# Half chunk's casts, masks, state sums and a gated load in the first stretch of a retention and mixer kernel

## The chip, the cores and the metric

The kernel runs on one core of a Trainium2 chip. Time is device time in microseconds (us) of that core. Executions of one kernel differ by up to 0.9% on one chip even at full clock.

## What it must compute

Retention (linear attention with a decay per head) for 8 batches, 8 heads, 576 rows, head size 64, and a token and channel mixer on its result.

```python
# attention: q, k, v are [8, 8, 576, 64]
scores = scale * q @ k^T
Dmat   = where(rel >= 0, gamma[h] ** rel, 0)          # rel = row - column
x      = ((scores * Dmat) @ v), heads joined          # [8, 576, 512]
# mixer
h  = (x^T @ U) @ V                                    # rank 32, over the rows
u  = x + h^T
out = u + relu(u @ w_ch1) @ w_ch2                     # 512 -> 2048 -> 512
```

## The kernel before

The batches are taken in pairs. A pair's 1152 rows make nine chunks of 128; chunk `J` is the **half chunk**, which has the last 64 rows of one batch and the first 64 of the next. The first pair has its own code, because nothing can be overlapped with it yet: its rows are taken as four **units** of 256 rows and two halves of the half chunk. The second pair starts with the "third batch"; its chunks come by the usual route: load, cast, transpose by DMA (`DMA_TRANSPOSE qkT<-qk`).

Names used below: `scale_u` and `cast_u` cast and scale a unit's queries, keys or values; `T_u` transposes them; `SC_u` makes scores, `SC_off` those between the two halves of a unit, `mask_u` masks them; `RV_u` multiplies with the values; `ST_u` adds to the running state, `Sblk` evicts it; `QS_u` multiplies queries with the state; `XS_u` scales the result. A **y item** is a group of matmuls of the first channel product (`u @ w_ch1`) with its evictions; PE has a list of them as filler. w1 and w2 stand for the weights `w_ch1` and `w_ch2`. `warm(n)` issues matmuls that only keep TensorE busy.

Three engine lists matter. ScalarE (ACT) does the evictions of transposed operands in the startup, GpSimd (POOL) casts and issues the weight loads, SyncE (SP) issues all other loads and the transposes.

```python
    def load(pr, i, which):
        c = ch.setdefault((pr, i), {})
        for j in which:
            if ("f", j) not in c:
                c["f", j] = stage.tile([P, H, D], FP32, tag="stage", name="stage_t")
            ...
                nc.sync.dma_start(out=c["f", j][rows, :, :], in_=...)
    ...
    def startup():
        load_u(0, (1, 0)) ...            # the loads of units 0, 1 and the half chunk
        warm(10)
        cast_unit(0)
        ...
        SC_u(0, 0, ps_sc, "psc")
        mask_u(0, 0)
        cast_unit(1)
        ...
        T_u(1, 1, nc.scalar)
        SC_u(0, 1, ps_o, "po")
        mask_u(0, 1)
        SC_off(0, ps_sc, "psc")
        warm(3)
        T_u(1, 0)
        nc.vector.memset(sblk, 0.0)
        SC_off(1, ps_o, "po")
        warm(3)
        SC_u(1, 0, ps_sc, "psc")
        mask_u(1, 0)
        cast_J(0, nc.scalar, nc.vector)  # half chunk: keys on ScalarE, queries on VectorE
        SC_u(1, 1, ps_o, "po")
        mask_u(1, 1)
        ...
        load_w1(10, 14)                  # 512 KB of w_ch1
        scale_u(3, 0, nc.gpsimd)         # unit 3's queries: scale and cast
        for hh in range(2):
            cast_u(3, 0, hh, nc.gpsimd)
        load_w1(14, 16)                  # the last 256 KB
        for hh in range(2):
            cast_u(3, 2, hh, nc.gpsimd)
        ...
    def first_stretch():
        ...
        for g in range(NI, NI + 4):      # the third batch's first 11 loads
            load(*order[g], (1, 0, 2) if g < NI + 3 else (1, 0))
        unit(2, (0, 1, 2), False)
        y(2)
        unit(3, (2, 3), True)
        for f in range(0, NF, 2):
            load_w2(f)                   # 2 MB of w_ch2
        ...
```

Of the kernel before, what the change touches and what calls it, by code (L numbers as in the profile page):

```python
# [34 lines left out]
def kernel(  # L35
# [81 lines left out]
    def early_consts():  # L117
        scratch = y1_pool.tile([P, NF, 4 * P], BF16, tag="y10", name="y1")
        un[0]["off"] = scratch[:, 0:4, :].rearrange("p (a x) (y i) -> p a (x y) i", x=2, i=P)
        tri = scratch[:, 4, 0:P]  # L120
        make_identity(nc, ident)
        nc.gpsimd.memset(lnb, math.log(scale))
        nc.gpsimd.iota(
            posU, pattern=[[2 * P, 4], [1, 2], [0, H]], base=0, channel_multiplier=2,
            allow_small_or_imprecise_dtypes=True,
        )
        nc.gpsimd.iota(
            iotaU, pattern=[[-1, 2], [1, P]], base=0, channel_multiplier=-2,
            allow_small_or_imprecise_dtypes=True,
        )  # L130
        nc.gpsimd.iota(
            pos, pattern=[[P, NI], [0, H]], base=0, channel_multiplier=1,
            allow_small_or_imprecise_dtypes=True,
        )
        nc.gpsimd.iota(
            posJ, pattern=[[-2 * J * P, 2], [0, H]], base=2 * J * P, channel_multiplier=1,
            allow_small_or_imprecise_dtypes=True,
        )
        make_upper_triangular(nc, tri, val=1.0, diag=True)
        nc.gpsimd.memset(triJ, 0.0)  # L140
        nc.gpsimd.affine_select(
            out=triJ, in_=triJ, compare_op=ALU.is_gt, fill=1.0, base=0,
            pattern=[[-2, HALF]], channel_multiplier=1)
        for h in range(H):
            nc.vector.memset(lngt[:, :, h], lng[h])
        nc.scalar.activation(out=Af[:, 0, 0:H], in_=lngt[:, 0, :], func=AF.Exp)
        nc.vector.tensor_copy(out=fan, in_=ident[0:R, None, 0:R].to_broadcast([R, 4, R]))
        nc.vector.tensor_scalar_add(posU[:, 2:4], posU[:, 2:4], -float(4 * P - HALF))
        nc.vector.tensor_tensor(
            out=posU.rearrange("p u j h -> p (u j) h"),  # L150
            in0=lngt[:, 0:8, :], in1=posU.rearrange("p u j h -> p (u j) h"), op=ALU.mult)
        nc.scalar.activation(out=vscaleU, in_=posU, func=AF.Exp, bias=lnb, scale=-1.0)
        nc.vector.tensor_scalar(
            out=posJ, in0=posJ, scalar1=0.5, scalar2=None, op0=ALU.mult)
        nc.vector.tensor_tensor(out=posJ, in0=posJ, in1=lngt[:, 0:2, :], op=ALU.mult)
        nc.scalar.activation(out=vscaleJ, in_=posJ, func=AF.Exp, bias=lnb, scale=-1.0)
        nc.scalar.activation(out=posJ, in_=posJ, func=AF.Exp, bias=0.0, scale=1.0)
        nc.vector.tensor_scalar(
            out=triU[0:HALF], in0=iotaU[0:HALF], scalar1=0.0, scalar2=None, op0=ALU.is_ge)
        nc.vector.tensor_scalar(  # L160
            out=triU[HALF:P], in0=iotaU[HALF:P], scalar1=-float(P), scalar2=None,
            op0=ALU.is_ge)
        nc.vector.tensor_scalar_add(pos[:, J + 1:NI, :], pos[:, J + 1:NI, :], -float(S))
        nc.vector.tensor_scalar_add(pos[HALF:P, J, :], pos[HALF:P, J, :], -float(S))
        nc.vector.tensor_tensor(out=lngt, in0=lngt, in1=pos, op=ALU.mult)
        nc.scalar.activation(out=qscale, in_=lngt, func=AF.Exp, bias=0.0, scale=1.0)
        nc.scalar.activation(out=vscale, in_=lngt, func=AF.Exp, bias=lnb, scale=-1.0)
        nc.vector.tensor_copy(out=triH[0:HALF], in_=tri[0:HALF, 0:HALF])
        nc.vector.tensor_copy(out=triH[HALF:P], in_=tri[HALF:P, HALF:P])
        nc.vector.memset(U_E[:, J, :], 0.0)  # L170
        nc.vector.memset(U_O[0:HALF, 0, :], 0.0)
        nc.vector.memset(V4[:, 0:HALF], 0.0)
        nc.vector.memset(V4[:, HALF + S:], 0.0)
        nc.vector.tensor_copy(out=swap[:, 0:HALF], in_=ident[:, HALF:P])
        nc.vector.tensor_copy(out=swap[:, HALF:P], in_=ident[:, 0:HALF])

    def load_u_rows():
        nc.sync.dma_start(
# [53 lines left out]

    ch = {}

    def load(pr, i, which):
        c = ch.setdefault((pr, i), {})
        for j in which:
            if ("f", j) not in c:
                c["f", j] = stage.tile([P, H, D], FP32, tag="stage", name="stage_t")
            dram = (q, k, v)[j]  # L240
            for rows, b, t0 in parts(pr, i):
                n = rows.stop - rows.start
                nc.sync.dma_start(
                    out=c["f", j][rows, :, :],
                    in_=dram[b, :, t0:t0 + n, :].rearrange("h s d -> s h d"),
                )
# [383 lines left out]
    def cast_u(u, j, hh, eng):  # L630
        o, f = unit_views(u, j, hh)
        if eng is nc.scalar:
            nc.scalar.activation(out=o, in_=f, func=AF.Copy)
        else:
            eng.tensor_copy(out=o, in_=f)  # L635
# [145 lines left out]
    def zero_J(x, eng):  # L781
        for j in range(3):
            t = stage.tile([P, H, D], FP32, tag="stage", name="stage_t")
            hj[x]["f", j] = t
            if eng is nc.scalar:
                nc.scalar.activation(
                    out=t.rearrange("p h d -> p (h d)"),
                    in_=ident[:, None, :].to_broadcast([P, 4, P]), func=AF.Copy, scale=0.0)
            else:
                eng.memset(t, 0.0)  # L790
# [118 lines left out]
    def startup():  # L909
# [12 lines left out]
        cast_unit(0)  # L922
        T_u(0, 1, nc.vector)
        nc.vector.memset(un[0]["off"][HI], 0.0)
        zero_J(1, nc.vector)
        load_J(1, (1, 0, 2))
        load_u(2, (1, 0, 2))
# [7 lines left out]
        cast_unit(1)  # L935
        cast_u(0, 2, 0, nc.gpsimd)
        cast_u(0, 2, 1, nc.gpsimd)
        cast_u(1, 2, 0, nc.gpsimd)
        load_w1(0, 2)
        cast_u(1, 2, 1, nc.gpsimd)  # L940
        T_u(1, 1, nc.scalar)
        SC_u(0, 1, ps_o, "po")
        mask_u(0, 1)
        SC_off(0, ps_sc, "psc")
        warm(3)
        T_u(1, 0)
        nc.vector.memset(sblk, 0.0)
        SC_off(1, ps_o, "po")
        warm(3)
        SC_u(1, 0, ps_sc, "psc")  # L950
        mask_u(1, 0)
        cast_J(0, nc.scalar, nc.vector)
        SC_u(1, 1, ps_o, "po")
        mask_u(1, 1)

        acc1 = pss_tile()
        ST_u(0, ALL, acc1, True)
        Sblk(acc1, 1)
        RV_u(0, 0)
        RV_u(0, 1)  # L960
        RV_off()
        XS_u(0)
        T_J(0)
        acc2 = ps_big.tile([P, NHP, P], FP32, tag="big", name="pss2")
        ST_u(0, ALL, acc2, True)
        prep_vJ(0)
        cast_urows()
        RV_u(1, 0)
        SC_J(0)
        mask_J(0)  # L970
        ST_u(1, LO, acc1, False)
        Sblk(acc1, 2)
        cast_J(1, nc.gpsimd, nc.gpsimd)
        load_w1(2, 4)
        prep_vJ(1)
        load_w1(4, 6)
        scale_u(2, 0, nc.gpsimd)
# [4 lines left out]
        load_w1(8, 10)  # L982
        for hh in range(2):
            cast_u(2, 2, hh, nc.gpsimd)
        load_w1(10, 14)
        scale_u(3, 0, nc.gpsimd)
        for hh in range(2):
            cast_u(3, 0, hh, nc.gpsimd)
        load_w1(14, 16)
        for hh in range(2):  # L990
            cast_u(3, 2, hh, nc.gpsimd)
        RV_u(1, 1)
        QS_u(1, 0, 1)
        XS_u(1, 0, 1)
        ST_u(1, ALL, acc2, False)
        Sblk(acc2, 3)
        QS_u(1, 1, 2)
        XS_u(1, 1, 2)
        RV_J(0)
# [33 lines left out]
    def first_stretch():  # L1033
# [3 lines left out]
        def y(n):  # L1037
            for _ in range(n):
                fn = next(ys, None)
                if fn is not None:  # L1040
                    fn()
# [13 lines left out]

        def unit(u, slots, last):
            T_u(u, 1, nc.vector)
            if last:
                y(1)
            T_u(u, 0)  # L1060
            y(1)
            SC_u(u, 0, ps_sc, "psc")
            mask_u(u, 0)
            y(1)
            ST_u(u, LO, acc, False)
            Sblk(acc, slots[1])
            SC_u(u, 1, ps_sc, "psc")
            mask_u(u, 1)
            if not last:
                scale_u(3, 1, nc.vector)  # L1070
            y(1)
            if not last:
                ST_u(u, HI, acc, False)
                Sblk(acc, slots[2])
            RV_u(u, 0)
            QS_u(u, 0, slots[0])
            QS_u(u, 1, slots[1])
            if last:
                RV_J(1)
                XS_J(1)  # L1080
            RV_u(u, 1)
            XS_u(u)

        for g in range(NI, NI + 4):
            load(*order[g], (1, 0, 2) if g < NI + 3 else (1, 0))
        unit(2, (0, 1, 2), False)
        y(2)
        unit(3, (2, 3), True)
        nc.vector.memset(w2_sb[:, 0, 0:1], 0.0)
        for f in range(0, NF, 2):  # L1090
# [78 lines left out]
```

## Time and profile before

| | before |
|---|---|
| time, median (range) | 326.98 us (326.25 to 327.29), 3 runs |
| span of the profiled execution | 323.8 us |
| PE busy | 312.6 us, 97% |
| PE idle before 70 us | 6.8 us |

PE works 97% of the time, so only the first 70 us have anything to win. The prediction below shows the page's busy row and the order of time of PE, ScalarE and SyncE there. First the chain of waits that ended last, as the page sums it up, each engine with its share of the span:

```profile
PE 77%; ACT 4%; DVE 2%; DMA 1%; issue 1%; DVEq 0%
```

Hardly any transfer is on that chain (1%). Second, the table by stage between 36 and 40 us; after the window and its length come busy us (and instructions) of PE, PEld, DVE, ACT and POOL, then the granted clock, the DMA share and GB/s:

```profile
36.00:38.00 2.00, 1.60 (x15) 0.94 (x13) 0.69 (x1) 1.07 (x2) 0.00 (x0) 1.00 1.22 224
38.00:40.00 2.00, 1.26 (x10) 0.65 (x10) 0.72 (x1) 0.86 (x2) 1.78 (x3) 1.00 0.90 201
```

The DMA engines move over 200 GB/s all that time. Third, SyncE's order of time at the last of the eleven early third-batch loads (start, length, what it issues):

```profile
49.57 5.39 SPq L243 DMA_DIRECT2D stage_t<-in_q_dram  x1
```

Of the loads before it, those issued after 40 us took SyncE 0.8 to 2.1 us each. This one took 5.39; it is the only one that had four of the w2 loads (issued from 46.9 us on, every 0.7 us) ahead of it. PE's line where the third batch begins, without a wait:

```profile
66.71 0.32 PE L296 MATMUL pp<-qkT 64*64 64x64 bf16 x16
```

### The profile page before, as it was taken

To read this page: it belongs to the slowest core of one execution; us is meant where nothing else is said; L and a number is where in the kernel's file an instruction comes from. 1 tells how busy PE (TensorE), PEld (TensorE's weight loads), DVE (VectorE), ACT (ScalarE), POOL (GpSimd) and SP (SyncE) were. 2 spreads that over 40 slices of the span, in tenths; PEclk is the share of its full clock that TensorE was granted. 3 is DMA by queue.
4 is the path that set the end of the run, shared out by engine and by line. 5 is a ranking of instruction groups with operands and counts; after the bars stand their busy time and mean duration, and the time that the engine had idled before them with its cause. 6 is when DMAs were issued, how large, how long until landed. Compare 5 with 4: busy or idle time off the path is not lost.

```text
span 323.8 us, 9143 instructions
## 1 busy us (share of the span) xinstructions
PE 312.6 (97%) x3885; PEld 170.8 (53%) x3885; DVE 172.9 (53%) x342; ACT 146.1 (45%) x334; POOL 101.5 (31%) x172
## 2 busy tenths in 40 slices
PE   7899899999999999999999999999999999999996
PEld 3575545764444454457644454457644454467544
DVE  7867456229726577555844476556744475500012
ACT  6757547892020583058800583058800572047400
POOL 7796329223113723052221523052231500010000
PEclk9999999999999999999999999999999999999999
DMA  7999999999975999979997599959996340330022
GB/s 215 256 233 255 227 216 185 201 188 127 254 180 139 232 193 187 213 147 190 197 205 166 140 184 206 217 140 189 182 217 156 100 68 3 107 105 0 2 78 84
DMA packets 152904, 53.30 MB, mean 165 GB/s; under 512 B 132032, under 2 KB 150336, under 8 KB 152864
## 3 DMA queue, kind: packets, MB, share of 16 engines
q1 hardware_dynamic: 144512, 40.40, 68.1%
q0 software_dynamic: 8352, 12.32, 15.9%
q8 instruction: 30, 0.49, 0.7%
q14 instruction: 10, 0.08, 0.1%
HBM read 36.85 MB, written 9.44 MB: 143 GB/s over the span
## 4 chain that ended last, share of the span: by engine, by line
PE 77%; ACT 4%; DVE 2%; DMA 1%; issue 1%; DVEq 0%
PE ps_y L549 37%; PE ps_y L515 32%; PE pp L296 2%; DVE u L464 2%; ACT y L520 1%; DMA qkT<-qk 1%; PE pp L316 1%; PE pp L328 1%; PE ps_y L560 1%; PE AB L358 1%; PE pa L431 1%; PE ph L458 1%; ACT s_sb L373 1%; ACT qk L264 0%; ACT uT L489 0%
## 5 line engine op out<-in xcount | busy, mean ns | idle before, releaser
L515 PE MATMUL ps_y<-uT,w_sb 128*128 128x256 bf16 (+2 forms) x768 | 133.1, 326 | 1.8 <-ACT y L520 1.1
L520 ACT ACTIVATE y<-ps_y 128x384 bf16<-128x384 f32 (+2 forms) x192 | 89.7, 491 | 96.6 <-PE ps_y L515 95.8
L549 PE MATMUL ps_y<-w_sb,y 128*128 128x512 bf16 x560 | 126.5, 380 | 0.0
L515 PEld LDWEIGHTS <-w_sb 128*128 128x128 bf16 x768 | 72.1, 98 | 49.6 <-issue 3.7
L549 PEld LDWEIGHTS <-y 128*128 128x128 bf16 x560 | 52.6, 98 | 61.1
L272 POOL TENSOR_TENSOR vt<-stage_t,vscale 64x256 bf16<-64x256 f32 (+1 forms) x81 | 50.4, 622 | 63.8 <-DMA stage_t<-in_v_dram 51.8
L538 DVE TENSOR_TENSOR o_sb<-ps_y,u 128x512 f32<-128x512 f32 (+2 forms) x38 | 25.2, 664 | 81.7 <-PE ps_y L549 79.4
L541 POOL DMA_DIRECT2D out_dram<-o_sb x31 | 17.2, 555 | 103.7 <-DVE o_sb L538 100.0
L304 DVE TENSOR_TENSOR ret<-pp,triH 128x512 bf16<-128x512 f32 x27 | 18.7, 692 | 24.6 <-PE pp L328 19.1
L464 DVE TENSOR_TENSOR u<-ph,xt 128x768 bf16<-128x768 f32 (+2 forms) x24 | 21.8, 951 | 5.9 <-PE ph L458 4.2
L437 ACT ACTIVATE a_sb<-pa 128x128 bf16<-128x128 f32 x8 | 2.2, 278 | 43.7 <-PE pa L431 43.7
L344 DVE TENSOR_TENSOR xt<-pp,qscale 128x512 bf16<-128x512 f32 x27 | 18.6, 690 | 4.7 <-PE pp L328 4.2
L338 DVE COPY q<-qkT 64x256 bf16<-64x256 bf16 x48 | 13.1, 272 | 13.7 <-DMA qkT<-qk 12.7
L263 DVE CAST qk<-stage_t 64x256 bf16<-64x256 f32 x54 | 18.8, 347 | 1.2
L383 DVE TENSOR_TENSOR s_sb<-AB,Af 64x256 bf16<-64x256 f32 x42 | 17.7, 422 | 2.1 <-ACT s_sb L378 1.5
L264 ACT ACTIVATE qk<-stage_t 128x512 bf16<-128x512 f32 x27 | 16.8, 622 | 0.0
L635 POOL CAST qk<-stage_t 128x512 bf16<-128x512 f32 x16 | 10.2, 637 | 11.4 <-DMA stage_t<-in_q_dram 6.6
L376 ACT ACTIVATE Af<-AB 128x256 f32<-128x256 f32 x24 | 9.2, 385 | 7.8 <-PE AB L358 7.4
L261 ACT ACTIVATE qk<-stage_t 128x256 bf16<-128x256 f32 x27 | 11.1, 410 | 0.0
L692 DVE TENSOR_TENSOR ret<-psc,triU 128x1024 bf16<-128x1024 f32 x8 | 9.6, 1206 | 2.6 <-PE psc L684 2.6
L296 PEld LDWEIGHTS <-qkT 64*64 64x64 bf16 x432 | 5.6, 107 | 9.8 <-issue 8.0
L209 PE MATMUL pw<-ident 128*128 128x512 bf16 x26 | 7.8, 443 | 1.4 <-POOL ident masks.py:199 1.4
(134 smaller groups left out, 220.0 us busy)
## 6 DMA issues: line engine op xcount, KB each, us to landing
stage_t<-in_k_dram SPq DMA_DIRECT2D x32, 256.0 KB, 4.9
stage_t<-in_q_dram SPq DMA_DIRECT2D x32, 256.0 KB, 5.4
stage_t<-in_v_dram SPq DMA_DIRECT2D x32, 256.0 KB, 5.6
out_dram<-o_sb POOLq DMA_DIRECT2D x31, 256.0 KB, 3.5
w_sb<-in_moe_w_ch_dram POOLq DMA_DIRECT2D x14, 256.0 KB, 8.3
stage_t<-in_k_dram SPq DMA_DIRECT2D x8, 128.0 KB, 3.7
stage_t<-in_q_dram SPq DMA_DIRECT2D x8, 128.0 KB, 3.7
stage_t<-in_v_dram SPq DMA_DIRECT2D x8, 128.0 KB, 3.9
```

Of the source, the lines that this page charges most:

```text
L263: nc.vector.tensor_copy(out=o[to, hl], in_=f[fr, hl])
L264: nc.scalar.activation(out=c["qk"][:, 0, :], in_=c["f", 0].rearrange("p h d -> p (h d)"), func=AF.Copy)
L272: nc.gpsimd.tensor_tensor(out=o[to, hl], in0=f[fr, hl], in1=w[fr, hl, :, None].to_broadcast([n, NHP, D]), op=ALU.mult)
L304: nc.vector.tensor_tensor(out=ret.rearrange("p a b i -> p a (b i)").rearrange("p a (b i) -> p a b i", i=D), in0=pp[:, :, 0:NHP * D].rearra ...
L344: nc.vector.tensor_tensor(out=st["x", pr][:, i, :].rearrange("p (hp hl d) -> p hl hp d", hl=2, d=D), in0=pp[:, :, NHP * D:2 * NHP * D].rea ...
L383: nc.vector.tensor_tensor(out=S_[half(x), 1, :], in0=Bk[half(1 - x)], in1=Af[half(1 - x), now, :], op=ALU.add)
L464: nc.vector.tensor_tensor(out=st["u", par][:, i0 - base:i0 - base + n, w].rearrange("p s (c d) -> p c s d", c=2), in0=ph[k][:, :, 0:n, :], ...
L515: nc.tensor.matmul(ps[:, 0:n, :], w1_sb[:, cc, f * P:(f + 1) * P], st["uT", par][:, c0:c0 + n, cc, :], start=(cc == 0), stop=(cc == NCC - 1),)
L520: nc.scalar.activation(out=st["y1", par][:, f, c0 * P:(c0 + n) * P], in_=ps[:, 0:n, :].rearrange("p s t -> p (s t)"), func=AF.Relu)
L538: nc.vector.tensor_tensor(out=o_sb[:, 0:n], in0=ps[:, 0:n], in1=st["u", par][:, c, w], op=ALU.add)
L541: (nc.sync if last else nc.gpsimd).dma_start(out=out_flat[r0:r0 + P, w], in_=o_sb[:, 0:n])
L549: nc.tensor.matmul(ps, st["y1", par][:, f, c * P:(c + 1) * P], w2_sb[:, f, :], start=(f == 0), stop=(f == NF - 1),)
```

## The change

Its intent: keep VectorE free for the masks in the startup (GpSimd scales the half chunk's queries, ScalarE copies constants, the masks of unit 1 come in a row, the state sums come early), and let w1 and unit 3 have the DMA engines before the third batch: its first load waits for a one-element memset that GpSimd reaches only after it has issued the last piece of w1. Cut to its core:

```diff
@@ early_consts: triangle and swap copies to ScalarE, memsets later; sblk's memset first
-    def load(pr, i, which):
+    def load(pr, i, which, gate=None):
...
+            if gate is not None:
+                gate.memset(c["f", j][:, 0:1, 0:1], 0.0)
@@ startup
         cast_u(0, 2, 0, nc.gpsimd)
         cast_u(0, 2, 1, nc.gpsimd)
+        cast_J(0, nc.scalar, nc.gpsimd)
         cast_u(1, 2, 0, nc.gpsimd)
...
         T_u(1, 0)
-        nc.vector.memset(sblk, 0.0)
         SC_off(1, ps_o, "po")
-        warm(3)
         SC_u(1, 0, ps_sc, "psc")
         mask_u(1, 0)
-        cast_J(0, nc.scalar, nc.vector)
-        SC_u(1, 1, ps_o, "po")
-        mask_u(1, 1)
         acc1 = pss_tile()
         ST_u(0, ALL, acc1, True)
         Sblk(acc1, 1)
+        SC_u(1, 1, ps_o, "po")
+        mask_u(1, 1)
+        acc2 = ps_big.tile([P, NHP, P], FP32, tag="big", name="pss2")
+        ST_u(0, ALL, acc2, True)
+        T_J(0)
...              # the other state sums ahead of RV_u(1, 0), too
-        load_w1(10, 14)
         scale_u(3, 0, nc.gpsimd)
         for hh in range(2):
             cast_u(3, 0, hh, nc.gpsimd)
+        load_w1(10, 14)
         load_w1(14, 16)
+        load(*order[NI], (1,), gate=nc.gpsimd)
...
         for g in range(NI, NI + 4):
-            load(*order[g], (1, 0, 2) if g < NI + 3 else (1, 0))
+            load(*order[g], ((0, 2) if g == NI else (1, 0, 2)) if g < NI + 3 else (1, 0))
         unit(2, (0, 1, 2), False)
-        y(2)
+        y(1)             # and in unit(): the y item between the two T_u for unit 2, too
```

**The early cast**: `cast_J`'s key half moves forward on ScalarE. **The gate**: the memset and the load behind it. **The late piece**: `load_w1(10, 14)` moves behind unit 3's queries.

More of the change, by code (lines that the diff above doesn't have):

```diff
@@ L157, in early_consts @@
         nc.scalar.activation(out=posJ, in_=posJ, func=AF.Exp, bias=0.0, scale=1.0)
+        nc.scalar.activation(out=triH[0:HALF], in_=tri[0:HALF, 0:HALF], func=AF.Copy)
+        nc.scalar.activation(out=triH[HALF:P], in_=tri[HALF:P, HALF:P], func=AF.Copy)
+        nc.scalar.activation(out=swap[:, 0:HALF], in_=ident[:, HALF:P], func=AF.Copy)
+        nc.scalar.activation(out=swap[:, HALF:P], in_=ident[:, 0:HALF], func=AF.Copy)
         nc.vector.tensor_scalar(
@@ L167, in early_consts @@
         nc.scalar.activation(out=vscale, in_=lngt, func=AF.Exp, bias=lnb, scale=-1.0)
-        nc.vector.tensor_copy(out=triH[0:HALF], in_=tri[0:HALF, 0:HALF])
-        nc.vector.tensor_copy(out=triH[HALF:P], in_=tri[HALF:P, HALF:P])
-        nc.vector.memset(U_E[:, J, :], 0.0)
-        nc.vector.memset(U_O[0:HALF, 0, :], 0.0)
-        nc.vector.memset(V4[:, 0:HALF], 0.0)
-        nc.vector.memset(V4[:, HALF + S:], 0.0)
-        nc.vector.tensor_copy(out=swap[:, 0:HALF], in_=ident[:, HALF:P])
-        nc.vector.tensor_copy(out=swap[:, HALF:P], in_=ident[:, 0:HALF])
+        nc.vector.memset(sblk, 0.0)
     def load_u_rows():
@@ L924, in startup @@
         nc.vector.memset(un[0]["off"][HI], 0.0)
+        nc.vector.memset(U_E[:, J, :], 0.0)
+        nc.vector.memset(U_O[0:HALF, 0, :], 0.0)
+        nc.vector.memset(V4[:, 0:HALF], 0.0)
+        nc.vector.memset(V4[:, HALF + S:], 0.0)
         zero_J(1, nc.vector)
@@ L937, in startup @@
         cast_u(0, 2, 1, nc.gpsimd)
+        cast_J(0, nc.scalar, nc.gpsimd)
         cast_u(1, 2, 0, nc.gpsimd)
+        cast_u(1, 2, 1, nc.gpsimd)
         load_w1(0, 2)
-        cast_u(1, 2, 1, nc.gpsimd)
         T_u(1, 1, nc.scalar)
@@ L958, in startup @@
         Sblk(acc1, 1)
+        SC_u(1, 1, ps_o, "po")
[3 more added lines that the diff above has]
+        T_J(0)
         RV_u(0, 0)
         RV_u(0, 1)
+        ST_u(1, LO, acc1, False)
         RV_off()
+        Sblk(acc1, 2)
         XS_u(0)
-        T_J(0)
-        acc2 = ps_big.tile([P, NHP, P], FP32, tag="big", name="pss2")
-        ST_u(0, ALL, acc2, True)
         prep_vJ(0)
         cast_urows()
-        RV_u(1, 0)
+        load_w1(2, 4)
         SC_J(0)
         mask_J(0)
-        ST_u(1, LO, acc1, False)
-        Sblk(acc1, 2)
+        ST_u(1, ALL, acc2, False)
+        Sblk(acc2, 3)
+        RV_u(1, 0)
         cast_J(1, nc.gpsimd, nc.gpsimd)
-        load_w1(2, 4)
         prep_vJ(1)
@@ L994, in startup @@
         XS_u(1, 0, 1)
-        ST_u(1, ALL, acc2, False)
-        Sblk(acc2, 3)
         QS_u(1, 1, 2)
@@ L1057, in unit @@
             T_u(u, 1, nc.vector)
-            if last:
-                y(1)
+            y(1)
             T_u(u, 0)
@@ L1084, in first_stretch @@
         for g in range(NI, NI + 4):
-            load(*order[g], (1, 0, 2) if g < NI + 3 else (1, 0))
+            load(*order[g], ((0, 2) if g == NI else (1, 0, 2)) if g < NI + 3 else (1, 0))
         unit(2, (0, 1, 2), False)
-        y(2)
+        y(1)
         unit(3, (2, 3), True)
```

## The prediction

> **What bounds the kernel now.** I read the page's shares first, then a table of each engine's busy time by stage, then the order of time of each engine in the first 75 us, and last the DMA issues with their landings. The page says where to look:
>
> ```profile
> span 323.8 us, 9143 instructions
> ...
> PE 312.6 (97%) x3885; PEld 170.8 (53%) x3885; DVE 172.9 (53%) x342; ACT 146.1 (45%) x334; POOL 101.5 (31%) x172
> ```
>
> TensorE (PE) is busy 97% of the span, so only 11.2 us are idle. The table by stage says where they lie:
>
> ```profile
> 10.00:20.00 10.00, 8.79 (x226) 6.59 (x215) 9.10 (x12) 6.28 (x12) 7.88 (x14) 1.00 1.11 224
> ...
> 80.00:100.00 20.00, 20.00 (x261) 9.42 (x260) 11.76 (x20) 2.31 (x6) 2.73 (x5) 1.00 0.91 205
> ```
>
> After the window and its length stand the busy times of PE, PEld, DVE, ACT and POOL. From 80 to 100 us PE has no gap at all; before 70 us it is idle 6.8 us (70 less the sum of seven PE figures, 63.2). All the change can win lies there, about 2%, less the 1.4 us at the start that nothing touches. DVE, busy 9.1 of 10 us between 10 and 20 us, is the other engine to watch. PE's order of time shows the gaps in brackets:
>
> ```profile
> 11.74 0.41 PE L726 MATMUL psx<-qkT 64*64 64x128 bf16 x8 [0.49 <-DVE ret L692]
> ...
> 13.63 0.82 PE L209 MATMUL pw<-ident 128*128 128x512 bf16 x3
> 14.38 0.86 PE L684 MATMUL psc<-qkT 64*64 64x128 bf16 x32
> ...
> 16.31 0.64 PE L711 MATMUL po<-qk,ret 64*128 64x64 bf16 x32 [0.52 <-DVE ret L692]
> ...
> 38.74 0.51 PE L655 MATMUL pst<-ident,qk 128*128 128x128 bf16 x6 [1.14 <-POOL qk L635]
> ```
>
> Two half-microsecond gaps wait for masks on DVE; 1.14 us waits for GpSimd's cast of unit 3's queries, which itself waits for their load. Here is what ScalarE does meanwhile:
>
> ```profile
> 9.51 0.70 ACT L202 ACTIVATE V<-pv 128x512 bf16<-128x512 f32 x2
> 10.94 1.02 ACT L667 ACTIVATE qkT<-pst 128x1024 bf16<-128x1024 bf16 x1 [0.72 <-PE pst L655]
> 12.19 1.02 ACT L730 ACTIVATE y<-psx 64x1024 bf16<-64x1024 f32 x1 [0.23 <-PE psx L726]
> 13.17 0.74 ACT L664 ACTIVATE qkT<-pst 128x512 bf16<-128x512 bf16 x1
> 13.78 0.99 ACT L730 ACTIVATE y<-psx 64x1024 bf16<-64x1024 f32 x1
> 14.67 0.62 ACT L809 ACTIVATE qk<-stage_t 128x512 bf16<-128x512 f32 x1
> ```
>
> The last line is the cast of the half chunk's keys, at 14.67, without a wait. The view of the line that loads them, cut to that one issue (8.17 us), says when they come:
>
> ```profile
> L796 SPq DMA_DIRECT2D stage_t<-in_k_dram x1: 782/782/782, 8.2 to 8.2; - x1
> ...
> DMA to landing us min/median/max: 5.2/5.2/5.2
> ```
>
> They land at 8.17 + 5.2 = 13.3 us. That is the number on which my prediction turns.
>
> **What the Trainium skill says.** "Perfetto Trace Analysis", section "Sequencer Loop": an engine takes its instructions one after another and each waits for its semaphores in its turn. So an early cast whose data is late holds up all of ScalarE behind it. The trace before has no such case there. "GPSIMD Engine Reference", section 3.1: a two-input fp32 operation is 1.96 times slower on GpSimd than on DVE. Here scaling 128x512 takes 1036 ns on POOL (values, L816) and 690 ns on DVE (queries, L805), a ratio of 1.5. "DMA: Bandwidth & Descriptors", section "Queues, rings and completion order": the DMA engines share themselves packet by packet among the queues that have work. The trace agrees: the third batch's last query load takes 16.1 us to land beside the w2 loads, against a median of 5.4. "TensorE: Matmul & The Clock Gate", Part 1: a fully idle window of some 3.4 us halves TensorE's clock. The trace agrees only in that the first ten warming matmuls take 0.37 us each (3.69/10), later ones 0.25 (1.24/5).
>
> **The change, part by part.** All by the order of instructions that the two programs give each engine, and by durations of the trace before.
>
> (1) Constants. Two triangle copies (1.03 and 0.63 us on DVE), two swap copies and four small memsets leave the front of DVE's list; the 0.91 us memset of the state blocks comes there. ScalarE takes the copies in its idle 1.71 us before the query scales: free. DVE evicts unit 0's keys at 6.5 instead of 7.01 and ends zeroing the second half chunk near 10.1 instead of 10.6. The first mask then starts when its scores are there (10.2 instead of 10.53), and the 0.49 us gap at 11.74 shrinks by 0.3.
>
> (2) DVE in the masks. The memset (14.26 to 15.1) and the query scaling (0.69 us at 16.17) are gone from between them: for DVE alone, the two masks of unit 1 could end 1 to 1.5 us sooner. GpSimd has time for the scaling: the queries land at 13.9 and its old wait for unit 1's values ran from 13.4 to 14.86; it is through with those values near 16.3, w1's first piece is issued at 16.3 instead of 15.4, and all later work keeps its time.
>
> (3) Three warming matmuls (0.65 us from start to next start) go. They stood in a wait anyway: what follows needs DVE's copy that ends at 14.1, and started at 14.38. Worth 0.2.
>
> (4) The cost. The key cast moves with the query scaling, and on ScalarE it now stands right after the two V copies, ahead of the eviction at 10.94. It cannot start before 13.35. ScalarE then runs: cast to 13.95, unit 1's keys to 14.95, first off-diagonal block to 15.9, query half to 16.65, second block to 17.55. Unit 1's scores need the third and the fourth: they start at 16.7 instead of 14.38, 2.3 us later, and PE stands idle about 3.2 us (13.4 to 16.7) where it was busy. Parts 1 to 3 win nothing back, for they end before this wait.
>
> (5) After it, PE does the same matmuls in another order: scores, state sum, scores, state sum, transposes, 48 small products, about 4.0 us, to 20.65. Then DVE scales unit 0's output (1.21), masks the half chunk (0.76), scales unit 1's first half (0.69): 23.3. Unit 1's second state product waits for that and starts at 23.35 against 21.00. The old gaps of 0.52 and 0.17 go, one of about 1.0 comes. The startup ends 2.3 us late.
>
> (6) What is absorbed: unit 3's queries are no later (the loads are in the same order), so the 1.14 us gap at 38.74 vanishes; one y item now stands between unit 2's two transposes and takes up the 0.34 us gap there. 2.3 - 1.14 - 0.3 = about 0.9 us remain.
>
> (7) The gate. Formerly the third batch's first load was issued early and stood in line:
>
> ```profile
> 30.51 3.34 SPq L243 DMA_DIRECT2D stage_t<-in_k_dram  x1
> ...
> 60.24 4.33 SPq L279 DMA_TRANSPOSE qkT<-qk  x1
> ```
>
> Now it waits for a memset that GpSimd reaches only after casting unit 3's queries (landed at 38.0; I estimate 37.3, because 0.5 MB of w1 no longer competes) and issuing w1's last 0.75 MB: 39.5. Between 39 and 41.5 the DMA engines lack work. Formerly they had by then moved nearly 1.3 of the eleven third-batch loads and most of w1 more: I estimate 0.4 MB behind, at some 200 GB/s about 2.1 us (1 to 3.4). All of it stays behind until w2 is through, since DMA runs full from 40 to 66 us. The first transpose of the third batch (issued at 60.24, landed 6.4 later at 66.6, just ahead of the PE use at 66.71) then lands near 68.7. PE would be there at 67.6 and wait 1.1. So the delay is the larger of 0.9 and 2.1, not the sum. The 0.65 us gap of PE at 69.64, behind ScalarE's evictions, partly goes since ScalarE catches up in that wait: -0.4.
>
> **Sum.** 2.3 lost at startup, 1.4 absorbed, 1.2 added at the third batch, 0.4 absorbed: +1.7 us, 326.98 + 1.7 = 328.7.
>
> **Rivals.** (a) The intended gain: the key cast doesn't hold ScalarE, because the load lands sooner. Then unit 1's scores start 0.5 us earlier and the mask gaps (0.5 + 0.5 + 0.2) go, while the query gap at 38.74 gives most of it back: 326.3. Against it: the loads ahead of the keys are unchanged and saturate DMA. (b) The gate costs nothing or helps, since w1 and unit 3 come sooner: then only step 6 stays, 327.9, or 327.2 if the third batch is not late at all and ScalarE's gap goes too. (c) The gate costs its full 3.4 us and comes with a late w1 for the eleventh y item (issue 38 plus 5 to 8 us, need about 43.3): 330.5 or more. (d) The idle 3.2 us trips TensorE's clock: some 3 us at half speed, +1.5: 330.2. It falls just short of the page's window, so I give it 15%.
>
> **Range and chances.** The cast's stall is nearly certain; how far slack absorbs it, and the gate, are not, by some 2 us each way: 326.0 to 331.2. Two per cent is 6.5 us: a gain of that needs all idle time before 70 us, a loss of that needs (c) and (d) together. Faster 0.02, same 0.95, slower 0.03.
>
> **What would show it.** In the changed profile: ScalarE's key cast near 13.4 after an idle of about 3 us that ends with a DMA; unit 1's scores on PE near 16.7 after a gap of about 3 us; unit 1's second state product near 23.3; no gap before unit 3's transposes; the first third-batch load issued near 39.5; the first third-batch transpose landing near 68.7, with PE waiting for it. The prediction is wrong if the key cast starts without a wait before 12, if unit 1's scores start before 15, or if the transpose lands by 67.

## The result and the profile after

| | before | changed |
|---|---|---|
| time, median (range), 6 runs each, same rounds | 326.31 us (325.39 to 327.29) | 329.69 us (328.76 to 330.92) |
| span of the profiled execution | 323.8 us | 328.2 us |

The ratio is 1.0102 (95% interval 1.0074 to 1.0131), so within 2%, on the slow side. Here and below, a ratio is the mean time of one kernel's fast runs over that of the other's of the same rounds, so not quite the ratio of the medians quoted. The time lies inside the predicted range, 1.0 us above the 328.7 that was predicted.

The page of the changed kernel (busy row, then the chain):

```profile
PE 310.3 (95%) x3857; PEld 170.7 (52%) x3882; DVE 171.6 (52%) x337; ACT 146.5 (45%) x338; POOL 102.2 (31%) x174
...
PE 74%; DMA 4%; ACT 3%; DVE 2%; issue 1%; DVEq 0%
```

PE's share of the chain is down by three points and DMA's is up by three: a transfer is now on the path. (PE's busy time is slightly understated: 25 matmul records of the second channel product are missing from this trace.) ScalarE's order of time in the startup:

```profile
10.02 0.70 ACT L199 ACTIVATE V<-pv 128x512 bf16<-128x512 f32 x2
13.92 0.63 ACT L808 ACTIVATE qk<-stage_t 128x512 bf16<-128x512 f32 x1 [3.21 <-DMA stage_t<-in_k_dram]
14.46 1.00 ACT L666 ACTIVATE qkT<-pst 128x1024 bf16<-128x1024 bf16 x1
...
16.27 0.72 ACT L663 ACTIVATE qkT<-pst 128x512 bf16<-128x512 bf16 x1
```

As foreseen, the key cast (second line) now stands ahead of the evictions of unit 1's transposes and holds them up for 3.21 us until its keys have landed; it starts at 13.92. VectorE does have the two masks in a row, in one group of two, but after an idle of 3.12 us. They start 2.4 us later than in the kernel before (15.09) and end 1.9 us later (19.85 against 17.99):

```profile
17.50 2.35 DVE L691 TENSOR_TENSOR ret<-psc,triU 128x1024 bf16<-128x1024 f32 x2 [3.12 <-PE psc L683]
```

PE's order of time, at the gaps named in the prediction:

```profile
12.01 0.41 PE L725 MATMUL psx<-qkT 64*64 64x128 bf16 x8 [0.27 <-DVE ret L691]
17.04 0.42 PE L683 MATMUL psc<-qkT 64*64 64x128 bf16 x16 [3.08 <-ACT qkT L663]
23.60 0.40 PE L745 MATMUL po<-sblk,qkT 128*128 128x128 bf16 x4 [0.97 <-DVE xt L753]
39.83 0.61 PE L654 MATMUL pst<-ident,qk 128*128 128x128 bf16 x8
70.93 0.32 PE L295 MATMUL pp<-qkT 64*64 64x64 bf16 x16 [2.60 <-DMA qkT<-qk]
```

Unit 1's scores start at 17.04 after 3.08 us of idle, against 14.38 before. The gap before unit 3's query transposes (1.14 us at 38.74) is gone (fourth line, no bracket). At 70.93, where the third batch's first score matmuls started at 66.71 without a wait, PE waits 2.60 us for the DMA transpose; without that wait it would have started at 68.33. So the startup's delay is partly absorbed on the way (1.6 us of 2.6 are left), and the transpose is later still and decides. The table by stage, and SyncE's order of time, show why it is late:

```profile
36.00:38.00 2.00, 2.00 (x51) 1.65 (x51) 1.19 (x3) 1.35 (x3) 0.95 (x2) 1.00 0.35 97
38.00:40.00 2.00, 2.00 (x20) 1.21 (x18) 1.67 (x2) 0.60 (x1) 2.00 (x5) 1.00 0.25 24
```

```profile
39.30 0.37 SPq L242 DMA_DIRECT2D stage_t<-in_k_dram  x1
...
51.41 5.38 SPq L242 DMA_DIRECT2D stage_t<-in_v_dram  x1
56.84 4.08 SPq L242 DMA_DIRECT2D stage_t<-in_k_dram  x1
60.96 5.86 SPq L242 DMA_DIRECT2D stage_t<-in_q_dram  x1
66.99 1.63 SPq L278 DMA_TRANSPOSE qkT<-qk  x1
```

From 36 to 40 us the DMA engines moved 97 and 24 GB/s instead of 224 and 201: 2 us times the differences is 0.25 + 0.35 = 0.6 MB left undone, worth 3 us at 200 GB/s. And then the delay grows; in this trace SyncE's order of time suggests how (e1 and e10 below show that this is not settled): the w2 loads begin at 48.5, and three of the eleven loads, not one, are still to be issued when five of them are ahead; they take SyncE 5.4, 4.1 and 5.9 us. SyncE reaches the transpose only at 66.99 (before: 60.24). It lands 3.9 us later, at 70.89, against 66.61: 4.3 us late.

### The profile page after: what moved, and what is told of

It reads as the page before. It is cut to its first block, busy times and chain, and to the rows that moved or that the text cites. A ratio compares the mean times of both kernels' runs of the same rounds, so it can differ in the third digit from the quotient of the medians.

```text
span 328.2 us, 9103 instructions
## 1 busy us (share of the span) xinstructions
PE 310.3 (95%) x3857; PEld 170.7 (52%) x3882; DVE 171.6 (52%) x337; ACT 146.5 (45%) x338; POOL 102.2 (31%) x174
## 4 chain that ended last, share of the span: by engine, by line
PE 74%; DMA 4%; ACT 3%; DVE 2%; issue 1%; DVEq 0%
PE ps_y L548 34%; PE ps_y L514 32%; DMA qkT<-qk 4%; PE pp L295 2%; DVE u L463 2%; ACT y L519 1%; PE pp L315 1%; PE ps_y L559 1%; PE pp L327 1%; PE AB L357 1%; PE pa L430 1%; PE ph L457 1%; ACT s_sb L372 0%; ACT uT L488 0%; PE pu L484 0%
## 5 line engine op out<-in xcount | busy, mean ns | idle before, releaser
L548 PE MATMUL ps_y<-w_sb,y 128*128 128x512 bf16 x535 | 123.8, 379 | 2.2 <-issue 1.1
L337 DVE COPY q<-qkT 64x256 bf16<-64x256 bf16 x48 | 14.2, 297 | 14.8 <-DMA qkT<-qk 13.8
L295 PE MATMUL pp<-qkT 64*64 64x64 bf16 x432 | 8.6, 198 | 3.9 <-DMA qkT<-qk 3.9
```

The costliest lines, as they stand in the source:

```text
L295: nc.tensor.matmul(pp[half(m), m ^ hl, hp * D:(hp + 1) * D], qkT[half(hl), NHP + hp, half(m)], qkT[half(hl), hp, half(m ^ hl)], start=True ...
L548: nc.tensor.matmul(ps, st["y1", par][:, f, c * P:(c + 1) * P], w2_sb[:, f, :], start=(f == 0), stop=(f == NF - 1),)
```

## The experiments

The reading to be tested: the early cast's delay and the gate's delay run side by side and the later of them sets the time, which here is the gate's. The rivals: only one of the two costs anything; they add; or something else in the change does it. Where the expectations use letters, A is that reading, and the letters after it are rivals.

Each kernel was timed in five rounds (6 runs). One table first. "Full clock" counts the runs whose mean granted clock was 1.0 or 0.999, "tripped" those at 0.995 or lower; each figure is the mean of those runs less the mean of the full-clock runs of the kernel before on the same chip (327.02, 326.38 and 325.82 us in calls 1, 2 and 3, and 326.37 for all six runs beside the first run of the changed kernel). The number of runs is in brackets. Runs in the slow state (one of e8, one of e13) are left out.

| kernel | cast | gate | late piece | other edits | median us | ratio (95%) | full clock | tripped |
|---|---|---|---|---|---|---|---|---|
| changed, first run | x | x | x | x | 329.69 | 1.0102 (1.0074 to 1.0131) | +3.3 (2) | +3.4 (4) |
| call 1: e1 | | x | x | x | 329.33 | 1.0063 (1.0028 to 1.0099) | +1.8 (5) | +3.7 (1) |
| e2 | x | | x | x | 328.75 | 1.0059 (1.0032 to 1.0087) | none | +1.9 (6) |
| e3 | | | x | x | 328.16 | 1.0042 (1.0013 to 1.0071) | +0.6 (2) | +1.7 (4) |
| e4 | | x | x | | 329.05 | 1.0061 (1.0029 to 1.0093) | +1.6 (3) | +2.3 (3) |
| call 2: e5 | x | | | | 327.79 | 1.0036 (1.0007 to 1.0066) | +0.2 (2) | +1.9 (4) |
| e6 | x | x | | x | 328.21 | 1.0039 (1.0016 to 1.0062) | +0.4 (2) | +1.9 (4) |
| e7 | | | | x | 325.56 | 0.9979 (0.9952 to 1.0007) | -0.5 (6) | none |
| e8 | | | | x, and more | 329.03 | 1.0087 (1.0046 to 1.0128) | +1.4 (1) | +3.4 (4) |
| call 3: e10, changed again | x | x | x | x | 328.55 | 1.0056 (1.0004 to 1.0108) | +1.6 (1) | +3.0 (5) |
| e11 | | x | | | 326.74 | 1.0011 (0.9962 to 1.0059) | +1.0 (6) | none |
| e12, e6 again | x | x | | x | 328.98 | 1.0063 (1.0009 to 1.0118) | +1.0 (2) | +3.6 (4) |
| e13 | | | | x, and more | 326.90 | 1.0000 (0.9946 to 1.0054) | +0.4 (4) | +1.6 (1) |

Two limits of this table. The changed kernel itself was 1.0% slower in its own rounds and 0.6% in call 3, so single ratios of a few tenths of a per cent are not firm. And a column with one to three runs says little. (A ratio leaves out the profiled run; the two columns by clock include it.) What follows rests on the traces first and on these times second.

### e1: the key cast back in its old place

```diff
-        cast_J(0, nc.scalar, nc.gpsimd)
+        cast_J(0, None, nc.gpsimd)          # queries only
...
         SC_off(1, ps_o, "po")
+        cast_J(0, nc.scalar, None)          # keys only
         SC_u(1, 0, ps_sc, "psc")
```

> The changed kernel with one instruction moved: ScalarE's cast of the half chunk's keys goes back behind the second off-diagonal eviction, the queries stay on GpSimd, the gate stays. Both theories: ScalarE no longer waits some 3 us near 10.7, unit 1's scores start on PE near 14.1 instead of 17.0, the first y item starts 2.5 to 3 us sooner than in the changed kernel (near 24.3). Theory A (the later of two arrivals counts: PE's, and the third batch's first transpose, which only the gate delays): the transpose still lands near 70.5 to 71, PE just waits longer for it (4 to 5 us instead of 2.6), and the time stays within 0.5 us of the changed kernel's, 329.2 to 329.7. Theory B (the startup stall and the gate's delay add up): the time falls by 1.5 us or more, to 328.2 or less.

The startup is fast again: unit 1's scores start at 14.35 (17.04 in the changed kernel), the first y item at 24.81 (27.09). The transpose lands at 70.66, as before within 0.2 us, and PE waits for it, as PE's order of time shows:

```profile
70.71 0.32 PE L295 MATMUL pp<-qkT 64*64 64x64 bf16 x16 [2.93 <-DMA qkT<-qk]
```

So the startup's gain of 2.3 us was not seen at 70 us. The wait was to be 4 to 5 us and was 2.93, because PE had waited another 1.39 us at 43.29 for a piece of w1. Measured: ratio 1.0063, which is 0.4% under the first run of the changed kernel and no less than its second (1.0056), so the times alone do not decide between A and B. By the trace the reading holds: with the transpose so late, the early cast is nearly hidden. The trace also shows a limit of the account above: from 36 to 40 us the DMA engines moved 226 and 25 GB/s, so the hole was 0.35 MB, little more than half of the changed kernel's, and the transpose was as late all the same. Again three loads (4.1 to 6.1 us each) were still to be issued beside w2.

### e2: no gate

```diff
-        load(*order[NI], (1,), gate=nc.gpsimd)
...
-            load(*order[g], ((0, 2) if g == NI else (1, 0, 2)) if g < NI + 3 else (1, 0))
+            load(*order[g], (1, 0, 2) if g < NI + 3 else (1, 0))
```

> The changed kernel without the gate: the third batch's first load waits for nothing but its buffer; w1's pieces stay in their new places, the early key cast stays. Theory A: the first transpose of the third batch lands near 66.5, PE comes to it near 68.3 and does not wait, and only the startup stall's remainder is left: 326.3 + 1.5 = 327.8 (327.3 to 328.3). Rival C (not the gate but the w1 pieces behind unit 3's queries delay the third batch): the transpose still lands at 69.5 or later and the time stays at 329 or more.

The transpose landed at 67.29, PE came to it at 69.72 and did not wait: here the startup decides. But PE was later than the mere 2.3 us of the startup allow. The table by stage shows the reason (the column after POOL is the granted clock):

```profile
16.00:17.00 1.00, 0.00 (x0) 0.00 (x0) 0.00 (x0) 1.00 (x3) 0.99 (x3) 0.99 0.69 154
17.00:18.00 1.00, 0.93 (x20) 0.76 (x20) 0.24 (x1) 0.88 (x2) 0.98 (x2) 0.50 0.86 188
...
21.00:22.00 1.00, 1.00 (x44) 0.90 (x35) 0.00 (x0) 0.85 (x3) 1.00 (x3) 1.00 1.03 300
```

After 2.82 us of idle, TensorE was granted half its clock from 17 to about 20.4 us; the 16 score matmuls took 0.64 us instead of 0.42. All six runs had a mean clock of 0.995. With the gate removed the ratio was 1.0059, against 1.0102 and 1.0056 in the two series of the changed kernel: what was expected, 327.8, was missed for a reason that nobody had put into it.

### e3: neither early cast nor gate

The edits of e1 and e2 together.

> Both undone: key cast late and no gate; all else as changed (memset and query scaling out of VectorE, state sums early, w1 behind unit 3's queries). Theory A: 326.0 (325.3 to 326.8), that is the kernel before or a few tenths better: the rest of the change wins about 0.5 us of startup, which unit 3's queries and the first transpose (landing near 66.5) take back. Rival D (the rest of the change is itself a loss, or a real gain that was hidden): 327.3 or more, or 325 or less.

Expected was the time of before; measured 1.0042. PE's order of time shows a third cause, of which e1 (1.39 us) and e4 (1.23 us, below) show a smaller form and the changed kernel none:

```profile
44.68 1.89 PE L514 MATMUL ps_y<-uT,w_sb 128*128 128x512 bf16 x4 [3.31 <-DMA w_sb<-in_moe_w_ch_dram]
```

PE waits 3.31 us for the piece of w1 that was moved behind unit 3's queries: issued at 37.6 instead of 29.94, it landed at 44.6 instead of 40.0. Right after that wait the four matmuls take 1.89 us in place of 1.04: half the clock again. So the late piece was to be tested by itself.

### e4: the kernel before with gate and late piece alone

```diff
-        load_w1(10, 14)
         scale_u(3, 0, nc.gpsimd)
         for hh in range(2):
             cast_u(3, 0, hh, nc.gpsimd)
+        load_w1(10, 14)
         load_w1(14, 16)
+        load(*order[NI], (1,), gate=nc.gpsimd)
```

> The kernel before with nothing but the gate and w1's 512 KB piece behind unit 3's queries. Theory A: the DMA engines fall to under 100 GB/s between 36 and 40 us, the first third-batch load is issued near 39.5, the first transpose lands near 70.5, PE waits 3.5 to 4.5 us for it, and the time is close to the changed kernel's: 326.3 + 3.0 = 329.3 (328.7 to 330). Theory B (delays add up, and the gate's own part is only what is left after the stall): 326.3 + 1.8 = 328.1 or less.

The transpose landed at 70.13, and PE waited for it, and 1.23 us for w1 at 43.30:

```profile
70.17 0.32 PE L298 MATMUL pp<-qkT 64*64 64x64 bf16 x16 [2.39 <-DMA qkT<-qk]
```

Ratio 1.0061, and +1.6 us in the full-clock runs. The startup is that of before, so these edits alone bring the late transpose and about as much loss as e1 (1.0063) and as e10, the changed kernel's second run. The wait was to be 3.5 to 4.5 us; with the 1.23 us for w1 it comes to 3.62.

### e5: the kernel before with the early cast alone

```diff
         cast_u(0, 2, 1, nc.gpsimd)
+        cast_J(0, nc.scalar, None)
...
-        cast_J(0, nc.scalar, nc.vector)
+        cast_J(0, None, nc.vector)
```

> The kernel before with nothing but the early key cast on ScalarE (queries stay on VectorE, no gate, w1 as before). By my step 4: ScalarE waits about 3 us for the keys near 10.5, unit 1's scores start near 17.0, PE idles about 3 us there, and unit 3's query gap of 1.1 us is gone in return: with TensorE's clock kept, 1.3 to 1.8 us more than before, ratio 1.004 to 1.0055. If the idle halves the clock as in the ungated run (about 3.4 us at half speed), 1.5 us more, ratio 1.009. Rival (the wait is hidden wholly by later slack): ratio under 1.002.

```profile
16.79 0.42 PE L684 MATMUL psc<-qkT 64*64 64x128 bf16 x16 [2.24 <-ACT qkT L664]
```

This is PE's line of unit 1's scores: 16.79 against 14.38, after an idle of 2.24 us (its warming matmuls were kept), with another 0.45 at 17.65. The granted clock then was 0.50 from about 18.8 to 22.2 us. The stall follows from the order of the program; only the profiled run shows it, but the times of the six runs go by the clock. The two runs at full clock took 326.59 and 326.62 us, 0.2 above before; the two at 0.994 and 0.995 took 327.99 and 327.60; the two at 0.989 took 328.80 and 328.91. Each step of 0.005 in the mean clock, 1.6 us of 326, costs 1.1 to 1.2 us. So, by two runs at full clock, the stall itself is absorbed almost wholly, and what the early cast costs is mostly the clock. One more thing in this trace: with neither gate nor late piece the transpose was issued at 62.74 and landed at 68.5, 1.9 us later than before; SyncE had been through with the early loads at 53.9 and waited for the casts ahead of the transpose. PE came at 69.21 and did not wait. So a late startup makes the transpose late as well.

### e6: the changed kernel with the piece of w1 back in its place

```diff
+        load_w1(10, 14)
         scale_u(3, 0, nc.gpsimd)
...
-        load_w1(10, 14)
         load_w1(14, 16)
```

> The changed kernel with w1's 512 KB piece issued ahead of unit 3's queries again, as before the change; gate and early key cast stay. If the gate makes the third batch late by leaving the DMA engines without work, this fills part of the hole: 100 GB/s or more between 36 and 40 us instead of 60, the third batch's first transpose lands 1 to 2 us sooner (69 to 70), time 0.5 to 1.5 us under the changed kernel's, ratio to before 1.005 to 1.008. If what counts is only when the gated load is issued (still after unit 3's queries, near 39.5 to 40), the transpose lands at 70.5 or later and the ratio stays at 1.010.

In the table by stage of this profile, the hole is gone although the gate stands (in e12, the same kernel again, it is not):

```profile
36.00:38.00 2.00, 2.00 (x49) 1.44 (x44) 1.39 (x2) 1.07 (x3) 1.11 (x3) 1.00 1.21 215
38.00:40.00 2.00, 2.00 (x22) 1.37 (x21) 1.31 (x2) 0.92 (x2) 0.61 (x1) 1.00 1.26 193
```

The gated load is issued at 37.1 instead of 39.3, one load instead of three is caught by w2 (6.0 us to issue), and the transpose lands at 67.87, sooner than the 69 to 70 expected. In PE's order of time there is no wait at it:

```profile
67.92 0.32 PE L295 MATMUL pp<-qkT 64*64 64x64 bf16 x16
```

### e7: the rest of the change

The edits of e3 and e6 together: neither early cast, gate nor late piece.

> What is left of the change when key cast, gate and w1 order are all as before: constants and state memset moved, queries scaled by GpSimd, masks in a row, state sums early, three warming matmuls fewer. The 3.31 us wait for w1 that the run with neither showed must be gone (the piece lands near 40, needed near 42.5). PE reaches the first y item near 24.3 instead of 24.5, unit 3's query gap takes that back, the first transpose lands near 66.6: ratio 0.998 to 1.001. Rival (the rest of the change is a loss of its own): ratio 1.003 or more.

All six runs were at full clock, the mean is 0.2% below before, and the interval contains 1. VectorE does its masks sooner (those of unit 1 from 14.68 to 17.03 instead of 15.09 to 17.99), but PE's first y item starts at 24.26 instead of 24.49, and at the third batch nothing of that is left:

```profile
66.67 0.32 PE L295 MATMUL pp<-qkT 64*64 64x64 bf16 x16
```

It was 66.71 before. In between PE has new waits: 0.97 us where the state product waits for the scaling `XS_u`, and 0.76 and 0.21 near 41 us for unit 3's casts, which depend on loads. The intended gain is a few tenths of a microsecond at most and cannot be told from nothing.

### e8: an attempt to keep the gain

e7 with both state products ahead of one scaling, more y items ahead of unit 3's transposes, and w2 loaded later.

```diff
         QS_u(1, 0, 1)
-        XS_u(1, 0, 1)
         QS_u(1, 1, 2)
-        XS_u(1, 1, 2)
+        XS_u(1)
...
-            y(1)
+            y(3 if last else 1)
...          # load_w2 moved behind some twenty y items, issued from 53.4 us
```

> A try at beating both: the former run, and both of unit 1's second products ahead of one scaling (takes the 0.97 us wait for VectorE away), two y items moved ahead of unit 3's query transposes (fills the 1.1 us wait there), w2's loads issued some 6 us later so that the third batch's transposes land sooner. If the waits found are the ones that count, PE reaches the third batch near 64.5 and the first transpose has landed by then: ratio 0.992 to 0.996. If the DMA engines bound this stage anyhow, the transpose lands at 66 or later, or w2 comes late for the second products near 71, and the ratio stays at 0.998 to 1.002.

A failure: 1.0087. The first y item came 1.3 us sooner (23.23), but the transpose, issued in good time at 60.87, landed only at 69.48, in company with the w2 loads, and PE waited 2.12 us for it.

### e10: the changed kernel again

> The changed kernel again, to stand on one chip beside the next two runs. Ratio 1.007 to 1.012; the third batch's first transpose lands near 71 and PE waits 2 to 3 us for it.

Ratio 1.0056 on this chip; the transpose landed at 70.88. In this profile the clock was at 0.50 from about 16.4 to 19.8 us, and the first y item started at 28.1, one microsecond later than in the first profile. Yet PE began at the third batch at 70.92, against 70.93 there: it waited 1.57 us for the transpose instead of 2.60. PE's line, and SyncE's:

```profile
70.92 0.32 PE L295 MATMUL pp<-qkT 64*64 64x64 bf16 x16 [1.57 <-DMA qkT<-qk]
63.73 5.14 SPq L278 DMA_TRANSPOSE qkT<-qk  x1
```

PE's line is the reading in short: what the startup loses is hidden behind the transpose, the tripped clock too (full 329.69, tripped 329.73 in the first six runs; one run of six at full clock here, too few to say). But SyncE's line contradicts the account of how the delay grows: here only two loads were caught beside w2 (3.2 and 8.0 us), SyncE issued the transpose 3.3 us sooner than in the first profile, and it landed at the same time, 7.2 us after its issue instead of 3.9. When SyncE gets to the transpose is thus not all that sets its landing; what the DMA engines still have to move by then may be. No run separates the two.

### e11: the kernel before with the gate alone

The gate's edits of e4 without moving the piece of w1.

> The kernel before with the gate and nothing else: w1's 512 KB piece stays ahead of unit 3's queries. If the gate by itself is what delays the third batch, its first transpose lands near 68, PE (which comes to it near 66.7) waits about 1.2 us, no wait for w1: ratio 1.003 to 1.005. If the gate is harmless once w1 is early: ratio under 1.002. If the gate alone does what gate and late w1 did together: ratio 1.006 and the transpose at 70.

```profile
68.46 0.32 PE L298 MATMUL pp<-qkT 64*64 64x64 bf16 x16 [0.85 <-DMA qkT<-qk]
```

The gated load is issued at 39.2, as in the changed kernel, but the transpose lands at 68.42: 1.8 us later than before and 2.5 sooner than in the changed kernel. PE waits 0.85 us here and 0.43 at the next chunk. The ratio (1.0011) is not told from 1; against the nine full-clock runs of before it is +1.0 us. All six runs kept the full clock.

### e12: e6 again, beside e10

> The changed kernel with w1's piece early, again, beside the changed kernel on one chip. If the order of w1 is worth what the first comparison across chips said, 0.4 to 0.7% under the changed kernel's ratio (so 1.003 to 1.006), with the first transpose near 68 and DMA above 180 GB/s between 36 and 40 us. If that was a difference of chips: ratio within 0.2% of the changed kernel's.

Expected to be faster than e10, it was not (medians 328.98 against 328.55): two runs at full clock took 326.58 and 326.98, the other four 328.95 to 330.22. In the profiled run the clock was at 0.50 from 16 to 22.7 us, and the first y item came at 29.32. The transpose landed at 69.56, not near 68, PE came at 70.50 and did not wait. With the transposes ahead of PE, nothing hides the tripped clock any more. The expectation had left the clock out. It also missed on DMA (above 180 GB/s was expected); the table by stage has a hole here:

```profile
36.00:38.00 2.00, 2.00 (x30) 1.01 (x28) 1.36 (x2) 1.36 (x3) 0.35 (x1) 1.00 1.01 173
38.00:40.00 2.00, 2.00 (x51) 1.58 (x50) 1.19 (x3) 1.36 (x3) 1.13 (x3) 1.00 0.32 55
```

The gated load was issued at 39.15, against 37.14 in e6. So the early piece makes the hole smaller, 0.4 MB against the 0.6 of the changed kernel, and closed it in only one of two profiles.

### e13: transposes issued earlier

e7 with the single scaling of e8, and the first two third-batch chunks cast and transposed some 11 us sooner, in the y items' stretch.

```diff
         y(1)
+        prep(NI)
+        load(*order[NI + 2], (2,))
         MH1(outs1[0])
         y(2)
+        prep(NI + 1)
```

> Second try at beating both: the rest of the change (late key cast, no gate, w1 early), both of unit 1's second products ahead of one scaling, and the third batch's first two chunks cast and transposed some 11 us sooner, ahead of the last loads in their queue, which stand behind w2. If the queue of loads is what holds the transposes, the first one lands by 56 and PE never waits for one; the gain is then the startup's, about 1 us: ratio 0.995 to 0.998. If the casts then hold up ScalarE or VectorE in the low-rank mixing near 47 to 52 us: ratio 1.000 or more.

Ratio 1.0000. The transposes were issued at 49.44 and 52.06 and landed at 61.97 and 66.67, that is after 12.5 and 14.6 us beside w2, just in time: PE did not wait at 67.24. But it waited 1.05 us at 41.70 and 0.85 at 53.04 for other operands. No version that was run beat the kernel before beyond the interval.

### The clock, over all runs

The early cast is in six of the timed series (changed kernel twice, e2, e5, e6, e12): the clock was below full in 27 of their 36 runs. Of the 33 runs of the kernel before in the three calls, of e7 and of e11, 45 runs of kernels whose profiles show no PE wait of more than 1.4 us, it was in 2. In e3 and e4, which have PE waits of 3.31 and 2.39 us further on, it was in 7 of 12; in e1, with 2.93 us, in 1 of 6; in e8, with 2.12 us, in 5 of 6, and in e13, with 1.05 us, in 2 of 6.

## Why the prediction was right, and where it was not

**Steps 1 to 3 (constants, masks, warming matmuls): right in kind, and too small to see.** The 0.49 us gap at 11.74 became 0.27, shrunk by 0.2 where 0.3 was written. The masks came in a row. The prediction let them win nothing because the cast's wait ends after them. e7 has these edits without that wait, and is not told from before either: its first y item comes 0.2 us sooner, and at the third batch nothing of that is left.

**Step 4 (the early cast): right.** Predicted: cast at 13.35, idle of PE about 3.2 us, unit 1's scores at 16.7. In the trace: 13.92, 3.08 and 17.04. The cast is half a microsecond later because its keys landed about that much later in this run (issued at 8.68 instead of 8.17, 5.2 us to land both times).

**Step 5: right.** A gap of about 1.0 us at 23.35 was predicted; 0.97 at 23.60 came.

**Step 6 (what is absorbed): right in kind, 0.4 us too much.** The 1.14 us gap vanished, but unit 2's 0.34 became 0.24, where 0.3 was to go, and a new wait of 0.24 came at 40.67. A startup 2.6 us late (first y item) was 1.6 us late at the token mixer's first product (46.63 became 48.19), where 0.9 was predicted from a start of 2.3: 1.0 was absorbed, not 1.4.

**Step 7 (the gate): right mechanism, wrong size.** The gated load was issued at 39.30 (39.5 predicted), DMA did go idle, and the later of the two delays, not their sum, set the time (e1 and e10 show it). The term of the sum was "2.1 us late, PE waits 1.1"; measured are 4.3 and 2.60, and 4.3 lies outside the 1 to 3.4 that was given for it. One thing was missed for certain, another probably. The hole was 0.6 MB and not 0.4, since it began at 36 us, where formerly the w1 piece ran: I had looked only at 39 to 41.5. And the shift was not passed on one to one: 0.6 MB are worth 3 us at 200 GB/s, and 4.3 came. In this trace loads pushed past 50 us fall among the w2 loads, and three issues of 4 to 6 us replace one. Whether that is the cause stays open: e1 speaks for it, with a smaller hole and the same three issues, e10 against it, with two such issues and the same landing.

The step also gave the gate what belongs to the late piece of w1. e11 has the gate without it: 1.8 us late and 0.85 us of wait, close to the 2.1 and 1.1 that I had estimated for "the gate". With the late piece as well, e4 and the changed kernel are 3.5 and 4.3 us late; with the gate and the early piece, e6 is 1.3 and its repeat e12 2.9, of which its later startup has a part that no run tells apart (e5: 1.9 from the early cast alone). I had named a late piece only as part of rival (c), where it would hurt a y item; e3 showed that hurt (3.31 us). In the changed kernel the 2.6 us late startup covers most of it, and no such wait is in its profile.

**Rival (d) (the clock): its chance was wrong.** It got 15%, because 3.2 us fell "just short of the page's window". (That the trace agreed with the page in its slow first matmuls was a weak reading: the granted clock stands at 1.00 there.) In 9 of 12 runs of the changed kernel the clock was below full, and idles of 2.24 and 2.82 us had been enough in e5 and e2. In the changed kernel this cost little in the first six runs, since the transpose was later anyway; without the gate it is most of what the early cast costs (e5). The counts of runs, and the half-clock windows, which follow a PE wait of 2.2 us or more in all six profiles that have one before 320 us (e2, e3, e4, e5, e10, e12), tie the clock to the idle; why one run of a kernel trips and the next does not is open.

**The size of the whole.** 328.7 was predicted and 329.69 measured in the first rounds. In the profile the predicted sum was +2.1 for the start of the third batch and -0.4 for the gap at 69.64. Measured there: +4.2 (66.71 became 70.93), -0.65 (the gap is gone), and +0.9 that had no term, since PE waits 0.18 and 0.69 us at the next two sections for their transposes. That makes +4.4, the difference of the two spans (328.2 less 323.8); in the medians it was +3.4. The second series gave 328.55. How much of the difference between these two is the chip and how much the draw of clocks is not settled. That the time fell inside the range owes something to its width of 5.2 us: the rise was predicted as 1.7 us and measured as 3.4 in the first rounds and 2.3 (in medians) in the second.

## What to carry to other kernels

ScalarE took its list in order here, and one cast that waited 3.21 us held up four evictions: before moving an instruction forward, look up when the transfer that feeds it lands, because what stands behind it will wait until then. Before delaying a load, see what else the DMA engines have to do in that window, and what the delayed load will then run beside; two shifts, a later load and a later weight piece, made a hole of 0.6 MB together, where the load alone made one of 0.2 (e11: 158 GB/s from 36 to 40 us, against 213). When several edits delay the same point, only the latest shows, and undoing one uncovers the next: test each alone on the old kernel, and write down the granted clock of every run, or the half-clock windows will be taken for the edit.

## What the Trainium skill lacked or had wrong

- "TensorE: Matmul & The Clock Gate", Part 1, gives about 3.4 us of full idleness as what halves the clock. Here idles of 2.24 us (e5, with another 0.45 us before the clock fell) and 2.82 us (e2) were followed by windows at 0.50 of some 3.4 us, while 3.08 us (changed kernel, first profile) and 2.93 us (e1) were not. As a safe bound for an idle the figure is too high.
- "DMA: Bandwidth & Descriptors", section "Queues, rings and completion order", says that engines share packet by packet, but has no figure for what this does to one transfer. Here the issue of a 256 KB load took SyncE 4.1 to 5.9 us beside the w2 loads in the changed kernel, against 0.8 to 2.1 us for those between 40 and 49 us in the kernel before, and a transpose took 12.5 us to land (e13) against 3.9 in the changed kernel.
- "GPSIMD Engine Reference", section 3.1, has 1.96 for a two-input fp32 operation against VectorE, measured on rows of 2048 elements. For rows of 512 with a bf16 result that is too high: the half chunk's query scaling took 1042 ns on GpSimd (changed kernel) and 691 ns on VectorE (before), a ratio of 1.5.
